# A last output sum in two column halves, sums moved ahead, and outputs behind an up product, in a RetNet and feed-forward kernel on one core

## The chip, the cores and the metric

The kernel runs on one core of a Trainium2 chip (trn2). The metric is the device time of one execution in microseconds (us); lower is better. The span in a profile is the time from the first to the last instruction; the measured time is some 1.8 us longer.

In the profile's lines PE is TensorE (matrix products), PEld its weight loads, DVE is VectorE, ACT is ScalarE, POOL is GpSimd and SP is SyncE; a name with q (SPq, ACTq) is that engine's issue of a transfer. In this kernel TensorE writes its products into banks of the memory PSUM; another engine copies them from there to a tile such as `sum` (0.69 us for VectorE's last copy, 128x512), and a transfer takes that to the output (256 KB land 2.0 us after issue, the median of 24). L462 is line 462 of the kernel that was run.

## The reference

A linear-attention recurrence makes rows of 512 numbers, and a feed-forward block with the activation `h - tanh(h)` follows:

```python
# q, k, v: 4 batches x 8 heads x 768 positions x 64, float32
for t in range(S):
    state = gamma * state + einsum('bhd,bhe->bhde', k[:, :, t], v[:, :, t])
    y[:, :, t] = scale * einsum('bhd,bhde->bhe', q[:, :, t], state)
x = y.transpose(0, 2, 1, 3).reshape(3072, 512)
h = x @ w_in                       # 512 x 2048
out = (h - tanh(h)) @ w_out        # 2048 x 512
```

## The kernel before

The positions are taken in 24 chunks of 128. The feed-forward part goes in 96 steps. A step is a tile `(n, m2)`: 256 rows `n` of x and 256 columns `m2` of the hidden layer. It has an "up" product into a PSUM bank, an activation of five ScalarE and six VectorE operations, and, two steps later (`LAG = 2`), a "down" product for each of two halves `j` of the rows. The down product adds up in a PSUM bank until the last tile of a group; then `add_up` empties the bank into the tile `sum`. The parts that the change touches:

```python
def shrink_multiply(n, m2):            # VectorE, three operations on h
    ...
def shrink_end(n, m2):                 # VectorE, three more; the last writes g
    ...

def down(n, m2, j, first, last):
    if first:
        o_p[j] = bank("o", f"o_{n}_{m2}_{j}")          # a pool of two banks
        keep_busy(o_p[j][:, :P])
    for i in range(2):
        nc.tensor.matmul(o_p[j], gT[n, m2][:, i, ts(j, P)], w2[:, 2 * m2 + i],
                         start=(first and i == 0), stop=(last and i == 1))

def add_up(n, m2, j):
    ...
    if j in begun:
        nc.vector.tensor_tensor(o, o_p[j], o, op=ALU.add)
    elif done and j % 2:
        nc.vector.tensor_copy(o, o_p[j])
    else:
        nc.scalar.copy(out=o, in_=o_p[j])
    begun.add(j)
    if done:
        nc.sync.dma_start(out=out[ds(n * TH + j * P, P)], in_=o)

def part(j, n, m2, first, last):
    down(n, m2, j, first, last)
    if last:
        add_up(n, m2, j)

def downs(lag):
    while len(waiting) > lag:
        tile_ = waiting.pop(0)
        for j in range(2):
            part(j, *tile_)

for s in range(BEGUN, len(steps)):
    n, m2, first, last = steps[s]
    ci = with_chunk.get(s)                 # every third step takes a chunk along
    if ci is not None:
        ...
        if ci >= FIRST:
            outputs_rest(ci)               # the chunk's last 16 small products into y
            keep_x(ci)                     # ScalarE: y -> xT
        if FIRST <= ci + 2 < NCH:
            products(ci + 2)
            mask(ci + 2)
            state(ci + 2)
        load_chunk(ci + 4)
        if FIRST <= ci + 1 < NCH:
            outputs(ci + 1)                # 48 small products into the same banks y
            see(ci + 1)
    ...
    for i in range(2):
        up(n, m2, i)
    waiting.append(steps[s])
    shrink_begin(n, m2)
    shrink_factors(n, m2)
    shrink_multiply(n, m2)
    shrink_end(n, m2)
    downs(LAG)
    ...
for j in range(2):
    for tile_ in waiting:
        part(j, *tile_)
```

## Time and profile before

| | before |
|---|---|
| device time, median of the first three runs | 755.27 us (754.33 to 755.91) |
| span of the profiled run | 752.6 us |
| TensorE busy | 739.6 us, 98% |
| VectorE, ScalarE busy | 69%, 52% |
| waits of TensorE after 100 us | three, 2.1 us together |

Two groups of instructions carry the kernel. The columns are line, engine, operation, tiles, shapes and count, then the busy time and the mean length of one in ns, then the idle time before them and what ended it:

```profile
L414 PE MATMUL h<-xT,w 128*128 128x256 f32 x1536 | 349.9, 381 | 0.3 <-DVE w L199 0.3
L462 PE MATMUL o<-w,g 128*128 128x512 f32 x768 | 345.6, 593 | 1.4 <-DVE sum L471 0.9 <-DVE g L453 0.5
```

They are the up and the down products, 695 of the 740 us. Each product written in the code is two rows here, since 96 steps with 8 up products make 768, not 1536. One row takes longer (381 ns) than its share of busy time (349.9 us / 1536 = 228 ns): they overlap. The last column is what a change can win without taking products away, and it is small. With TensorE at 98% there is little to win in the other engines' own time. What is left is the few spots where TensorE stands still, and the end, where everything else has to come after it.

### The profile page before, as it was taken

How to read it: one execution, taken by the hardware profiler on the slowest of the kernel's cores; microseconds unless marked ns; L12 is line 12 of the kernel's file. 1: busy time of each engine (PE TensorE's matmuls, PEld its weight loads, DVE VectorE, ACT ScalarE, POOL GpSimd, SP SyncE). 2: the span in 40 equal slices, each digit the busy share in tenths (PEclk: the TensorE clock that was granted, in tenths of full speed). 3: DMA queues.
4: the chain of work that ended last, by engine and by line, in shares of the span. 5: the costliest groups of instructions: out<-in, count | busy, mean ns of one | idle time of the engine just before them, and what ended most of it. 6: DMA issues, size and time to landing. Idle time of an engine off the chain costs nothing.

```text
span 752.6 us, 13801 instructions
## 1 busy us (share of the span) xinstructions
PE 739.6 (98%) x5470; PEld 501.9 (67%) x5470; DVE 518.7 (69%) x807; ACT 389.1 (52%) x725; POOL 125.9 (17%) x108
## 2 busy tenths in 40 slices
PE   7899999999999999999999999999999999999997
PEld 7786666666667676766676666666666666666663
DVE  4899889998898666656565656555665566556653
ACT  3667486666665545445545545444344434433441
POOL 0564445435453111100111100000000000000000
PEclk9999999999999999999999999999999999999999
DMA  9982546556553353332442422000000000000000
GB/s 191 231 204 59 127 99 180 149 148 160 149 128 91 92 140 115 88 82 78 106 99 74 96 57 58 28 1 1 29 0 1 28 1 0 29 0 1 28 2 28
DMA packets 125392, 59.76 MB, mean 79 GB/s; under 512 B 109840, under 2 KB 118160, under 8 KB 125328
## 3 DMA queue, kind: packets, MB, share of 16 engines
q1 hardware_dynamic: 125184, 58.73, 30.5%
q8 instruction: 43, 0.70, 0.4%
q10 hardware_dynamic: 144, 0.15, 0.1%
q14 instruction: 21, 0.17, 0.1%
HBM read 35.80 MB, written 14.68 MB: 67 GB/s over the span
## 4 chain that ended last, share of the span: by engine, by line
PE 94%; DVE 2%; DMA 1%; SPq 1%; ACT 1%; issue 1%; DVEq 0%; ACTq 0%
PE h L414 43%; PE o L462 43%; PE y L352 3%; PE s L298 2%; PE s L304 1%; DMA raws<-in_moe_w_in_dram 1%; PE kqTp L250 1%; DMA k<-in_k_dram 1%; SPq L229 1%; PE kqTp L212 0%; DVE head L185 0%; PE y L212 0%; SPq L154 0%; DVE head L183 0%; DVE g L453 0%
## 5 line engine op out<-in xcount | busy, mean ns | idle before, releaser
L414 PE MATMUL h<-xT,w 128*128 128x256 f32 x1536 | 349.9, 381 | 0.3 <-DVE w L199 0.3
L462 PE MATMUL o<-w,g 128*128 128x512 f32 x768 | 345.6, 593 | 1.4 <-DVE sum L471 0.9
L414 PEld LDWEIGHTS h<-xT,w 128*128 128x128 f32 x1536 | 289.7, 190 | 71.1 <-issue 34.0
L462 PEld LDWEIGHTS o<-w,g 128*128 128x128 f32 x768 | 145.4, 190 | 145.7 <-issue 136.6
L423 ACT ACTIVATE u<-h 128x512 f32<-128x512 f32 x96 | 57.3, 597 | 292.0 <-PE h L414 291.9
L439 DVE TENSOR_TENSOR th<-h,th 128x512 f32<-128x512 f32 x96 | 66.3, 690 | 176.0 <-ACT th L424 175.9
L453 DVE COPY_PREDICATED g<-large,th 128x512 f32<-128x512 int32 x96 | 72.1, 751 | 10.6 <-ACT apart L273 0.5
L442 DVE SCALAR_TENSOR_TENSOR h<-q,h 128x512 f32<-128x512 f32 x96 | 66.9, 696 | 10.4 <-DVE h L440 0.5
L448 DVE SCALAR_TENSOR_TENSOR h<-q,h 128x512 f32<-128x512 f32 x96 | 66.8, 696 | 9.9
L431 ACT ACTIVATE q<-u,tab 128x512 f32<-128x512 f32 x96 | 69.4, 723 | 0.0
L432 ACT ACTIVATE q<-u,tab 128x512 f32<-128x512 f32 x96 | 69.0, 718 | 0.0
L433 ACT ACTIVATE large<-u,tab 128x512 f32<-128x512 f32 x96 | 68.7, 716 | 0.0
L452 DVE TENSOR_TENSOR g<-h,u 128x512 f32<-128x512 f32 x96 | 66.3, 691 | 3.3
L440 DVE SCALAR_TENSOR_TENSOR h<-u,h 128x512 f32<-128x512 f32 x96 | 65.8, 685 | 0.0
L424 ACT ACTIVATE th<-h 128x512 f32<-128x512 f32 x96 | 56.8, 591 | 0.0
L236 POOL TENSOR_TENSOR q<-q,tab 128x512 f32<-128x512 f32 x22 | 23.2, 1057 | 199.7 <-DMA q<-in_q_dram 113.5
L195 POOL TENSOR_TENSOR low<-low,power 128x512 f32<-128x512 f32 x30 | 38.7, 1290 | 102.2 <-DVE power L187 80.6
L199 POOL TENSOR_TENSOR w<-low,head 128x512 f32<-128x512 f32 x30 | 38.5, 1284 | 2.4
L352 PEld LDWEIGHTS y<-a,v 64*64 64x64 f32 x768 | 15.8, 134 | 17.2 <-ACT large L433 10.6
L236 POOL TENSOR_TENSOR v<-v,tab 128x512 f32<-128x512 f32 x22 | 26.5, 1206 | 0.2 <-DMA v<-in_v_dram 0.2
L352 PE MATMUL y<-a,v 64*64 64x64 f32 x768 | 21.1, 224 | 2.3 <-issue 1.8
L382 ACT COPY seen<-y 64x1 f32<-64x1 f32 x96 | 10.1, 154 | 25.3 <-PE y L352 24.9
(49 smaller groups left out, 374.4 us busy)
## 6 DMA issues: line engine op xcount, KB each, us to landing
rows<-apart SPq DMA_DIRECT2D x16, 512.0 KB, 2.6
k<-in_k_dram SPq DMA_DIRECT2D x24, 256.0 KB, 4.0
q<-in_q_dram SPq DMA_DIRECT2D x24, 256.0 KB, 4.9
v<-in_v_dram SPq DMA_DIRECT2D x24, 256.0 KB, 5.3
raw<-in_moe_w_out_dram SPq DMA_DIRECT2D x12, 512.0 KB, 3.5
out_dram<-sum SPq DMA_DIRECT2D x24, 256.0 KB, 2.0
raw<-in_moe_w_in_dram SPq DMA_DIRECT2D x14, 256.0 KB, 4.2
raw<-in_moe_w_in_dram SPq DMA_DIRECT2D x28, 128.0 KB, 3.9
```

What stands on the lines that cost most here:

```text
L352: nc.tensor.matmul(y[ds(D * col, D), r, p // 2, ts(a, D)], lhsT, rhs, start=start, stop=True, skip_group_check=True)
L414: nc.tensor.matmul(hp, w1[:, c, ts(2 * m2 + i, P)], xT[n // 2][:, c, ts(n % 2, TH)], start=(i == 0 and c == 0), stop=(c == NC - 1), skip_g ...
L431: nc.scalar.activation(q0, u, AF.Square, bias=bias0)
L432: nc.scalar.activation(q1, u, AF.Square, bias=bias1, scale=math.sqrt(A))
L433: nc.scalar.activation(large, u, AF.Relu, bias=bias_m)
L439: nc.vector.tensor_tensor(th, hp, th, op=ALU.subtract)
L440: nc.vector.scalar_tensor_tensor(hp, in0=u, scalar=R, in1=hp, op0=ALU.subtract, op1=ALU.mult, reverse0=True)
L442: nc.vector.scalar_tensor_tensor(hp, in0=q0, scalar=C0, in1=hp, op0=ALU.add, op1=ALU.mult)
L448: nc.vector.scalar_tensor_tensor(hp, in0=q1, scalar=A * C1, in1=hp, op0=ALU.add, op1=ALU.mult)
L452: nc.vector.tensor_tensor(flat, hp, u, op=ALU.mult)
L453: nc.vector.copy_predicated(flat, large.bitcast(I32), th)
L462: nc.tensor.matmul(o_p[j], gT[n, m2][:, i, ts(j, P)], w2[:, 2 * m2 + i], start=(first and i == 0), stop=(last and i == 1))
```

## The change

The intent has four pieces. The sums are issued ahead of the activation's last three vector operations, so that PSUM banks come free sooner. The last chunk's outputs go behind an up product, so that this fills the wait for `keep_x`. At the end the waiting tiles are done one by one. And the second output sum of the last 256 rows is made in two column halves, each in its own bank, so that the first half can be copied and sent while the second is still being summed.

```diff
+    def down_half(n, m2, j, c, first, last):
+        if first and c == 0:
+            o_p[j] = banks("t", f"o_{n}_{m2}_{j}")       # one tile of two banks
+        for i in range(2):
+            nc.tensor.matmul(o_p[j][:, c, :TH], gT[n, m2][:, i, ts(j, P)],
+                             w2[:, 2 * m2 + i, ts(c, TH)],
+                             start=(first and i == 0), stop=(last and i == 1))
+
+    def store_half(n, j, c):
+        o = sums[n][0][:, j]
+        at = out[ds(n * TH + j * P, P)]
+        if c == 0:
+            nc.scalar.copy(out=o[:, :TH], in_=o_p[j][:, c, :TH])
+            nc.sync.dma_start(out=at[:, :TH], in_=o[:, :TH])
+            return
+        for quarter, copy, queue in (
+            (2, nc.vector.tensor_copy, nc.sync),
+            (3, nc.scalar.copy, nc.scalar),
+        ):
+            cols = ts(quarter, P)
+            copy(out=o[:, cols], in_=o_p[j][:, c, ts(quarter - 2, P)])
+            queue.dma_start(out=at[:, cols], in_=o[:, cols])
...
     def part(j, n, m2, first, last):
+        if n == 2 * NB - 1 and j == 1:
+            for c in range(2):
+                down_half(n, m2, j, c, first, last)
+                if last:
+                    store_half(n, j, c)
+            return
...
-            if FIRST <= ci + 1 < NCH:
+            if FIRST <= ci + 1 < NCH - 1:
                 outputs(ci + 1)
                 see(ci + 1)
...
             up(n, m2, i)
+        if ci == NCH - 2:
+            outputs(ci + 1)
+            see(ci + 1)
         waiting.append(steps[s])
...
         shrink_multiply(n, m2)
+        downs(LAG)
         shrink_end(n, m2)
-        downs(LAG)
...
-    for j in range(2):
-        for tile_ in waiting:
-            part(j, *tile_)
+    downs(0)
```

## The prediction

> **What bounds the kernel now.** I read the busy shares first, then the row of slices, then TensorE's waits, then the timeline around each wait.
>
> The page's busy shares and its TensorE row of 40 slices:
>
> ```profile
> PE 739.6 (98%) x5470; PEld 501.9 (67%) x5470; DVE 518.7 (69%) x807; ACT 389.1 (52%) x725; POOL 125.9 (17%) x108
> PE   7899999999999999999999999999999999999997
> ```
>
> TensorE is busy 98% of the span, at granted clock 1.0; only the first two and the last slice are below 9. So every microsecond that can be won without taking matmuls away is an idle spell of PE, and there are about 13 us of them (752.6 minus 739.6), mostly in the first 45 us, which the change doesn't touch. The view of PE's waits from 100 us to the end has only three entries (total, times, longest):
>
> ```profile
> PE o L462 <- DVE sum L471: 0.9, 1, 0.9
> PE y L352 <- ACT xT L393: 0.7, 1, 0.7
> PE o L462 <- DVE g L453: 0.5, 1, 0.5
> ```
>
> Each occurs once, and each part of the change aims at one. The timeline shows all three (start, length, engine, line, in brackets the idle time before). First, near 144 us:
>
> ```profile
> 139.83 3.62 PE L414 MATMUL h<-xT,w 128*128 128x256 f32 x16
> 142.95 0.73 DVE L453 COPY_PREDICATED g<-large,th 128x512 f32<-128x512 int32 x1
> 143.57 1.28 DVE L471 TENSOR_TENSOR sum<-o,sum 128x512 f32<-128x512 f32 x2
> 144.30 3.70 PE L462 MATMUL o<-w,g 128*128 128x512 f32 x8 [0.86 <-DVE sum L471]
> ```
>
> The new down product needs the PSUM banks that two sums still have to empty, and VectorE reaches these only after the last activation operation of the tile. Second, at the last chunk's outputs:
>
> ```profile
> 490.48 0.46 PE L352 MATMUL y<-a,v 64*64 64x64 f32 x16
> 491.01 0.59 ACT L393 COPY xT<-y 128x512 f32<-128x512 f32 x1 [0.94 <-PE y L352]
> 491.65 0.69 PE L352 MATMUL y<-kqT,state 64*64 64x64 f32 x32 [0.71 <-ACT xT L393]
> ```
>
> Earlier chunks have another chunk's products in this place; the last has none. Third, the end, with the row of output transfers (KB each, us from issue to landing) from the page:
>
> ```profile
> 737.68 5.31 PE L462 MATMUL o<-w,g 128*128 128x512 f32 x12
> 742.73 0.73 DVE L453 COPY_PREDICATED g<-large,th 128x512 f32<-128x512 int32 x1
> 743.51 5.42 PE L462 MATMUL o<-w,g 128*128 128x512 f32 x12 [0.51 <-DVE g L453]
> 748.96 0.69 DVE L473 COPY sum<-o 128x512 f32<-128x512 f32 x1 [5.51 <-PE o L462]
> out_dram<-sum SPq DMA_DIRECT2D x24, 256.0 KB, 2.0
> ```
>
> After PE ends (748.93) come 0.69 us of copy, a transfer issued at about 749.68 that lands 2.0 us later (751.65), and about 0.95 us of closing.
>
> [...]
>
> **The change part by part.** I also read the built program's list of instructions and waits of both kernels.
>
> *Sums ahead.* Same instructions, moved. In the step near 144 us the third activation operation ends at about 141.3; two sums of 0.68 us then end at about 142.7. PE wants the banks at 139.83 + 3.46 = 143.29 and began at 144.30. Gain 1.0 us, plus about 0.05 of restart. The activation tile comes later by up to 1.4 us in these steps, but is used two steps (more than 4 us) after it is due.
>
> *Outputs behind the up product.* Before, this spot costs 492.57 - 490.55 = 2.02 us between products of the main loop, plus 0.2 because an up product after small products takes 3.65 us and not 3.45: 2.22. After: the 16 small products cost 0.39 + 0.2 (as at 513.43 to 513.82); the 48 others, at 14.6 ns each (112 more products cost 1.64 us more at 467.7 to 469.7), cost 0.70, plus about 0.16 to enter and 0.2 to leave: 1.06. Sum 1.65. Gain 0.55 us.
>
> *The end.* Tile-wise order gives PE the second output of tile 6 to do while tile 7's activation ends. PE needs tile 7 at about 737.68 + 16 x 0.429 = 744.55, and it was ready at 743.46, so the 0.68 us of lost issue (743.51 minus 737.68 + 12 x 0.429) go, and PE unhindered would end at 748.25. But the list of waits holds a catch: the first product of the second half waits for ScalarE's semaphore at the count that the copy of the **first half** gives. The halves are in different banks of one tile, and PE stands still nonetheless. First half ends at 748.25 - 0.86 = 747.39; copy of 256 columns 0.02 + 0.37, wake 0.05, four passes of 216 ns and 0.19 of pipe: 748.88. PE's end hardly moves. Next, the list makes ScalarE's last quarter wait for VectorE's quarter [...]: 0.02 + 0.27 + 0.03 + 0.27 + 0.03, so the last transfer is issued at about 749.50, not 749.68. It carries 64 KB and not 256; I estimate 1.65 us to landing (a quarter of the bytes, in rows of 512 bytes, beside a twin): 751.15 instead of 751.65. Gain 0.5 us.
>
> *Split matmuls.* 8 tiles, each 8 passes of 216 ns for 4 of 429: 0.012 us each, so 0.1 us lost at most.
>
> Sum: 1.05 + 0.55 + 0.5 - 0.1 = 2.0 us. 755.27 - 2.0 = **753.3 us**.
>
> **The rivals.**
> R1, the end works as intended: PE doesn't stand still between the halves. Then it ends near 748.3, the quarters overlap, and the gain at the end is about 1.3 instead of 0.5: 752.4. For it: separate banks. Against it: the wait stands in the built program.
> R2, the wait turns up elsewhere: with sums ahead, VectorE blocks until the down product is complete, and the activation comes late. 17 later sum steps losing 0.3 us each would make 5 us, 758. For it: VectorE is at 8 to 9 tenths in slices 6 to 12. Against it: no step after 144 us shows any PE wait for an activation tile until the last one, so there is slack of steps, and PE's matmuls in these sums are nearly done when VectorE gets there.
> R3, small transfers land no sooner, or the last three queue behind each other (512 KB leave in about 2.5 us now, where the first 256 KB had 3.5 us of their own): last landing 2.0 us or more after issue, gain at the end 0 to 0.2, so 753.7.
> R4, half-width passes are slower than in the up product, by weight loads of 190 ns in a slot of 216: 25 ns on 64 passes are 1.6 us, 754.9. Against it: 16 up passes keep 216 with the same loads.
>
> **Range and chances.** The gains are 0.9 to 1.1, 0.3 to 0.7 and 0 to 1.3 us, which gives 752.4 to 754.1; three runs of the kernel before spread over 1.6 us, so I widen it to 752.0 to 754.8. Two per cent are 15 us; the idle spells the change can reach are 2.1 us of PE and some 3.7 us after it, so faster by 2% can't come about. Slower by 2% would need R2 at more than 0.5 us in every sum. Chances: 0.005 faster, 0.99 same, 0.005 slower.
>
> **What would show each step right or wrong.** PE's waits after 100 us should have lost the first two entries, and the one for the activation tile, and should have gained one of about 0.4 us: PE for ScalarE's copy of the half sum, near the end; without it R1 holds. The down product after the first sum should start 3.46 us after its up product. Last quarters: VectorE's, then ScalarE's, about 0.27 us each, end to end. The last transfer should land about 1.65 us after its issue; 2.0 or more is R3. Half-width passes of the down product spaced by more than 220 ns are R4. New PE waits for g or h between 150 and 500 us are R2, and would make the prediction wrong on the high side.

On the inputs of these sums: the spacing of the rows is from the chain of before, where an up product of 16 rows takes 3.45 us (216 ns a row of 256 columns) and a down product of 8 rows 3.43 us (429 ns a row of 512). The copy lengths for 128 and 256 columns (0.27 and 0.37 us) and the 1.65 us to landing were estimates. For the copies the trace of before can be asked: ScalarE's take 154 ns for one column (`seen`) and 582 for 512 (`sum`), VectorE's 418 for 256 (`state`) and 681 for 512, and straight lines through these give 0.26 and 0.37 us on ScalarE and 0.29 on VectorE. The changed kernel has 0.27 and 0.37 on ScalarE, 0.29 on VectorE, and 1.6 us to landing for 64 KB. That 64 KB would land sooner than the 2.0 us of 256 KB was not shown by the trace of before.

## The result

| | before | changed |
|---|---|---|
| median of 6 runs | 754.7 us (754.06 to 755.91) | 752.89 us (752.56 to 753.87) |
| span of the profiled run | 752.65 us | 752.06 us |

The ratio is 0.9977, with a 95% interval of 0.9964 to 0.9989. A ratio is the mean time of one kernel's fast runs over that of the other's in the same rounds, so it isn't quite the ratio of the medians in the table. All outputs are right.

The two profiled spans differ by 0.6 us only, the medians by 1.8. The profiled run of the changed kernel was the slowest of its six, and what it lost, it lost before the change acts. This is the table by stretches, for the stretch from 30 to 40 us (busy time and count for PE, PEld, DVE, ACT and POOL, then the granted TensorE clock, the DMA share and GB/s). First before, then changed:

```profile
30.00:40.00 10.00, 8.29 (x166) 7.29 (x167) 8.41 (x15) 6.27 (x14) 6.66 (x6) 1.00 0.91 253
```

```profile
30.00:40.00 10.00, 7.87 (x157) 7.10 (x158) 8.63 (x14) 5.74 (x13) 6.77 (x6) 0.83 0.83 241
```

The clock fell to 0.83 there. Both programs issue the same instructions in this stretch, so this differs by execution and not by kernel (in e5_apart and e8_apart_scalar below, whose clock stayed at 1.00, TensorE came to its main loop late as well, so the clock is not the whole cause). Why it fell is not shown; TensorE's longest idle spell there was 2.9 us. One and the same up product early in the main loop began at 132.94 us before and at 134.43 in the changed kernel. Over the ten profiles its start lies between 132.85 and 134.95 us. I therefore measure the effects from this product on: the **main stretch** from it to the start of the last up product, and the **end** from there to the end of the span.

| | main stretch | end | both, against before |
|---|---|---|---|
| before | 734.23 - 132.94 = 601.29 us | 18.42 us | |
| changed | 734.06 - 134.43 = 599.63 us | 18.00 us | 1.66 + 0.42 = 2.08 us less |

The end is read from the table by stretches, which gives it to 0.01 us; the span as the page prints it is rounded to 0.1 us. (The expectations below were written with ends taken from rounded spans, 18.37 and 18.04 us.) Before, then changed:

```profile
734.23:752.65 18.42, 14.18 (x41) 7.33 (x39) 6.92 (x10) 3.50 (x6) 0.00 (x0) 0.98 0.07 28
```

```profile
734.06:752.06 18.00, 14.22 (x53) 9.61 (x51) 6.53 (x10) 4.13 (x8) 0.00 (x0) 1.00 0.08 29
```

Each stretch comes from one profile per kernel. Kernels that are alike in a stretch agree closely there: the three with the end of before (18.40 to 18.42) and the three with the changed end (17.99 to 18.00) within 0.02 us, and the main stretches of five kernels with all of the change's main part within 0.01.

Now the lines that answer to those of before. The page's busy shares and TensorE's slices of the changed kernel:

```profile
PE 740.9 (99%) x5502; PEld 509.9 (68%) x5502; DVE 518.0 (69%) x807; ACT 389.4 (52%) x727; POOL 126.9 (17%) x108
PE   8899999999999999999999999999999999999997
```

TensorE has 32 rows more (5502 against 5470), the halves. The view of its waits from 100 us to the end has one entry in place of three:

```profile
PE o L470 <- ACT sum L478: 0.5, 1, 0.5
```

The timeline at the first sum:

```profile
141.31 3.62 PE L414 MATMUL h<-xT,w 128*128 128x256 f32 x16
142.71 1.28 DVE L495 TENSOR_TENSOR sum<-o,sum 128x512 f32<-128x512 f32 x2
143.91 0.69 DVE L448 SCALAR_TENSOR_TENSOR h<-q,h 128x512 f32<-128x512 f32 x1
...
144.77 1.45 PE L462 MATMUL o<-w,g 128*128 128x512 f32 x3
```

The sums (L495 now) end before the up product does, and the down product follows 3.46 us after the up product began; before it was 4.47. The timeline at the last chunk's outputs:

```profile
490.84 0.46 PE L352 MATMUL y<-a,v 64*64 64x64 f32 x16
491.23 3.72 PE L414 MATMUL h<-xT,w 128*128 128x256 f32 x16
491.37 0.58 ACT L393 COPY xT<-y 128x512 f32<-128x512 f32 x1 [0.94 <-PE y L352]
...
494.88 0.69 PE L352 MATMUL y<-kqT,state 64*64 64x64 f32 x32
```

ScalarE's copy to xT now lies inside the up product, and there is no bracket at the second row of small products. The end:

```profile
744.40 1.88 PE L462 MATMUL o<-w,g 128*128 128x512 f32 x4
746.12 1.03 PE L470 MATMUL o<-w,g 128*128 128x256 f32 x4
...
747.18 0.37 ACT L478 COPY sum<-o 128x256 f32<-128x256 f32 x1 [0.28 <-PE o L470]
...
747.61 1.13 PE L470 MATMUL o<-w,g 128*128 128x256 f32 x4 [0.46 <-ACT sum L478]
748.83 0.29 DVE L486 COPY sum<-o 128x128 f32<-128x128 f32 x1 [5.54 <-DMA out_dram<-sum]
...
749.15 0.27 ACT L486 COPY sum<-o 128x128 f32<-128x128 f32 x1 [1.60 <-DVE sum L486]
749.45 0.35 ACTq L487 DMA_DIRECT2D out_dram<-sum  x1
```

The last tile no longer waits for its activation. In its place there is a new wait in the middle of the last output: the second half (L470 at 747.61) starts only when ScalarE has copied the first (747.18 + 0.37). The two last quarters are copied one after the other, 748.83 and 749.15, on two engines. (For the bracket at 748.83 the profile names a transfer as the releaser. The last one issued before, at 746.93, took 2.0 us and landed only after the copy had begun, so it can't have released it; the copy follows TensorE's end at 748.74.)

### The profile page after: what moved, and what is told of

Its sections match the earlier page's. It is cut to its first block, busy times and chain, and to the rows that moved or that the text cites. A ratio compares the mean times of both kernels' runs of the same rounds, so it can differ in the third digit from the quotient of the medians.

```text
span 752.1 us, 13885 instructions
## 1 busy us (share of the span) xinstructions
PE 740.9 (99%) x5502; PEld 509.9 (68%) x5502; DVE 518.0 (69%) x807; ACT 389.4 (52%) x727; POOL 126.9 (17%) x108
## 4 chain that ended last, share of the span: by engine, by line
PE 96%; DMA 2%; DVE 1%; SPq 1%; ACT 0%; issue 0%; ACTq 0%; DVEq 0%
PE h L414 44%; PE o L462 42%; PE y L352 3%; PE o L470 2%; PE s L298 2%; PE s L304 1%; PE kqTp L212 1%; PE kqTp L250 1%; DMA raw<-in_moe_w_in_dram 1%; DMA k<-in_k_dram 1%; SPq L229 1%; DMA out_dram<-sum 0%; SPq L154 0%; DVE power L187 0%; DVE head L185 0%; DVE a L311 0%
## 5 line engine op out<-in xcount | busy, mean ns | idle before, releaser
L462 PE MATMUL o<-w,g 128*128 128x512 f32 x736 | 331.9, 593 | 0.0
L462 PEld LDWEIGHTS o<-w,g 128*128 128x128 f32 x736 | 139.4, 190 | 135.1 <-issue 128.4
L393 ACT COPY xT<-y 128x512 f32<-128x512 f32 x24 | 14.1, 587 | 17.0 <-PE y L352 17.0
```

## The experiments

The first four kernels ran on one chip and share nine runs of the kernel before (median 754.76 us), and the last four likewise (754.8 us). Since a start that differs by up to 2 us lies on every time, I read each effect from the profile's stretches, and use the times as a check.

**e1_sums**: the kernel before, with the sums moved alone.

```diff
-        shrink_end(n, m2)
         downs(LAG)
+        shrink_end(n, m2)
```

> The kernel before with the sums moved ahead of the activation's last three operations, and nothing else. Theory (the sum of independent gains): the idle spell of 0.86 us at the first sum goes, the down product there starts 3.46 us after its up product and not 4.47; the other two late waits of PE (0.7 for the xT copy, 0.5 for the activation tile at the end) stay. Time 1.0 us less than before, ratio about 0.9987. Rival (VectorE blocks in its sums and hands its waits on): the wait is gone but new PE waits for g or h turn up between 150 and 500 us, and the time is the same as before or longer.

Median 753.3 us of 5, ratio 0.9985 (0.9973 to 0.9998). The first wait is gone, the other two are there, and no new one came. The main stretch is 733.04 - 132.87 = 600.17 us, 1.12 less than before; the end is 18.40, as before within 0.02. The rival falls.

**e2_outputs**: the kernel before, with the last chunk's outputs moved alone.

```diff
-            if FIRST <= ci + 1 < NCH:
+            if FIRST <= ci + 1 < NCH - 1:
...
+        if ci == NCH - 2:
+            outputs(ci + 1)
+            see(ci + 1)
```

> The kernel before with only the last chunk's outputs moved behind an up product. Theory: the wait of 0.71 us for the xT copy goes, but the small products leave a dense stretch twice instead of once (0.2 us each), so the stretch from the down product before to the one after is shorter by 0.55 us and not by 0.9. Time 0.55 us less, ratio about 0.9993. Rival (the whole wait is won): 0.7 us or more less in that stretch.

Median 754.34 us of 5, ratio 0.9996 (0.9984 to 1.0009): as a time, inconclusive. The profile is not. The chain of work that ended last (start, length, what) shows the spot before:

```profile
490.55 0.44 PE y L352 x16
...
491.65 0.93 PE y L352 x48
492.57 3.65 PE h L414 x16
496.23 3.43 PE o L462 x8
499.66 3.45 PE h L414 x16
```

and in this run:

```profile
492.13 0.39 PE y L352 x16
492.52 3.65 PE h L414 x16
496.17 0.86 PE y L352 x48
497.03 3.63 PE o L462 x8
500.66 3.45 PE h L414 x16
```

From the first small products to the next step's up product it takes 500.66 - 492.13 = 8.53 us, against 499.66 - 490.55 = 9.11. So 0.58 us are won of a wait of 0.71. The rest is seen in the lengths: the down product took 3.43 us when it followed an up product and takes 3.63 after small ones. The rival, the whole wait, falls. The main stretch is 600.71 us, 0.58 less than before.

**e3_end**: the kernel before, with only the end changed (`downs(0)`, `down_half` and `store_half`).

```diff
-    for j in range(2):
-        for tile_ in waiting:
-            part(j, *tile_)
+    downs(0)
     # and part(), down_half(), store_half() as in the change
```

> The kernel before with only the end changed: tile by tile order and the last output in two halves. Theory: from the start of the last up product to the end of the span 18.0 us as in the changed kernel, against 18.37 before; PE's wait for the copy of the first half is there with about 0.5 us. Time 0.35 us less than before, ratio about 0.9995. Rival (the end works as meant and the rest of the change is worth little): 17.4 us or less, and the time 1 us less.

Median 754.45 us of 5, ratio 0.9998 (0.9985 to 1.0012). As a time this is inconclusive. The end is 17.99 us, 0.43 less than before, and has the wait for the first half, 0.5 us. The main stretch is 601.38 us, 0.09 longer, about what six steps with half-width products were expected to cost. The whole end is thus worth 0.34 us, and the rival falls.

**e4_whole**: the changed kernel, with the last output kept whole.

```diff
-        if n == 2 * NB - 1 and j == 1:
+        if False and n == 2 * NB - 1 and j == 1:
```

> The changed kernel with the last output kept whole (512 columns, one copy, one transfer of 256 KB); sums, outputs and the tile by tile order stay. Theory (the halves cost a PE stall of about 0.6 us and the last quarters run one after the other, so the halves win nothing): from the start of the last up product to the end 17.75 us, 0.3 us less than the changed kernel's 18.04; time the same as the changed kernel's or 0.3 us less. Rival (the halves carry the gain at the end): 18.4 us or more, time 0.5 us or more above the changed kernel's.

Median 752.82 us of 5, ratio 0.9975 (0.9962 to 0.9987). The main stretch is 732.89 - 133.30 = 599.59 us; that is 1.70 less than before, and the 1.12 and 0.58 of the first two runs add up to it. The end is 17.63 us. Its timeline:

```profile
736.34 10.46 PE L462 MATMUL o<-w,g 128*128 128x512 f32 x24
...
746.84 0.69 DVE L497 COPY sum<-o 128x512 f32<-128x512 f32 x1 [4.73 <-PE o L462]
```

All 24 rows run without a gap, and one copy and one transfer follow. This end is 0.37 us shorter than that of the changed kernel. The tile-wise order alone brings 18.42 - 17.63 = 0.79 us; the halves, as built, give 0.37 of it back. In the times this is too small to be seen (0.9975 against 0.9977).

**e5_apart**: the changed kernel, with the halves in two PSUM tiles.

```diff
-        if first and c == 0:
-            o_p[j] = banks("t", f"o_{n}_{m2}_{j}")
+        if first:
+            o_half[c] = banks("t", ...)[:, 0] if c == 0 else bank("o", ...)
```

> The changed kernel with the two column halves in two separate PSUM tiles (the second in a bank of the pool of the whole outputs, free by then) instead of two banks of one tile; copies and transfers as in the changed kernel. Theory (the stall between the halves comes from the wait kept for the tile, not from the banks): PE's 0.5 us wait for the copy of the first half is gone, PE's last product ends 0.73 us sooner, and from the start of the last up product to the end it takes 17.3 us (17.5 if the transfers get in each other's way) against 18.04. Rival (the end is held by the transfers, not by PE): the wait is gone, but that stretch stays above 17.9 us.

Median 752.18 us of 5, ratio 0.9963 (0.995 to 0.9975). TensorE has no wait after 100 us. The timeline of the end:

```profile
745.41 1.03 PE L472 MATMUL o<-w,g 128*128 128x256 f32 x4
...
746.27 1.03 PE L472 MATMUL o_1b<-w,g 128*128 128x256 f32 x4
746.48 0.37 ACT L480 COPY sum<-o 128x256 f32<-128x256 f32 x1 [0.28 <-PE o L472]
...
747.34 0.29 DVE L488 COPY sum<-o_1b 128x128 f32<-128x128 f32 x1 [4.75 <-PE o_1b L472]
```

The second half starts 0.86 us after the first (1.49 in the changed kernel), and ScalarE copies the first half while the second is being summed. The end is 17.20 us, 0.80 shorter than the changed kernel's and 0.43 shorter than with the output whole. The rival, that transfers hold the end, falls.

**e6_apart_single**: the same, but the second half leaves in one VectorE copy and one transfer.

```diff
-        for quarter, copy, queue in (...):        # two copies, two transfers
-            ...
+        nc.vector.tensor_copy(o[:, TH:], o_half[c][:, :TH])
+        nc.scalar.dma_start(out=at[:, TH:], in_=o[:, TH:])
```

> As the run with separate tiles, but the second half leaves in one VectorE copy of 256 columns (about 0.42 us) and one transfer of 128 KB instead of two quarters on two engines. Theory (the quarters run one after the other, 0.29 + 0.27 and 0.03 between[...]; and 128 KB land only 0.1 us later than 64): the stretch from the last up product to the end is the same as with quarters within 0.1 us, 17.2 to 17.3. Rival (two engines and two queues are worth something): 0.25 us or more longer than with quarters.

Median 751.72 us of 5 (751.49 to 751.87), ratio 0.9958 (0.9945 to 0.997). The end is 17.19 us, the same as with quarters (17.20). Two engines and two queues were worth nothing here: one copy took 0.42 us where two in turn take 0.29 + 0.03 + 0.27, and 128 KB landed 1.7 us after issue where 64 KB took 1.6. Why the program lets the second quarter's copy wait for the first was not tested: the two share a bank, and also a PSUM tile.

**e7_sums_first**: the changed kernel, with the sums still further ahead.

```diff
+        downs(LAG)
         shrink_multiply(n, m2)
-        downs(LAG)
         shrink_end(n, m2)
```

> The changed kernel with the sums moved further ahead, before all six vector operations of the activation. Theory (the activation tile has about 4 us of slack, but VectorE is nearly full until 300 us): VectorE stands waiting for the down product in each sum step, about 3 us; after 300 us, where it is half idle, PE still waits for nothing; before 300 us VectorE falls behind and PE waits between 1 and 15 us in all. Rival (there is no slack to speak of, and the sums as changed were just lucky): PE waits in the seven late sum steps too, and the time is 10 us or more above the changed kernel's.

Median 753.22 us of 4, ratio 0.9974 (0.9959 to 0.9989). My expectation for the time before 300 us was wrong: TensorE has no wait at all after 100 us but the one between the halves. The view of VectorE's waits from 50 us on shows what the place of the sums costs that engine:

```profile
DVE sum L497 <- PE o L462: 34.5, 7, 6.0
DVE sum L495 <- PE o L462: 19.2, 12, 3.5
```

VectorE stands for 53.7 us in its sums, and all of it is hidden. (In the changed kernel the same two rows have 1.6 us together.) The main stretch is 599.64 us, the changed kernel's within 0.01. The rival, that there is no slack, falls with even more room than I had given the theory.

**e8_apart_scalar**: as e6_apart_single, with VectorE on the first half and ScalarE on the second.

```diff
-            nc.scalar.copy(out=o[:, :TH], in_=o_half[c][:, :TH])      # c == 0
-        nc.vector.tensor_copy(o[:, TH:], o_half[c][:, :TH])           # c == 1
+        cols = ts(c, TH)
+        (nc.vector.tensor_copy, nc.scalar.copy)[c](out=o[:, cols], in_=o_half[c][:, :TH])
+        (nc.sync, nc.scalar)[c].dma_start(out=at[:, cols], in_=o[:, cols])
```

> As the run with one copy and one transfer for the second half, but VectorE copies the first half and ScalarE the second (0.37 us, against about 0.42 on VectorE, and it issues the transfer itself). Theory: 0.05 to 0.15 us shorter at the end than with VectorE, 17.1 to 17.2 us from the last up product; time 1.0 us less than the changed kernel's, 0.9962 of the kernel before. Rival (the end is set by the first transfers, 256 and 128 KB, still under way): no difference.

Median 752.14 us of 5 (751.66 to 752.55), ratio 0.9963 (0.9951 to 0.9976). The end is 17.11 us, 0.08 less than with VectorE's copy, as expected; the rival falls, if by little. The time was not lower. In the two profiled runs (752.44 and 751.49 us) the later start, 133.88 against 132.85 at the product that I measure from, is more than the difference; that the start parts the medians too is not shown. By profile this is the best end; by time e6_apart_single is the best kernel. Which of the two is better stays open, since the start varies by more than what parts them. Both beat the kernel before (intervals below 1) and have a shorter end than the changed one.

The stretches of all runs, in us:

| | main stretch | end | less than before, both | ratio of times |
|---|---|---|---|---|
| before | 601.29 | 18.42 | | 1 |
| changed | 599.63 | 18.00 | 2.08 | 0.9977 |
| e1_sums | 600.17 | 18.40 | 1.14 | 0.9985 |
| e2_outputs | 600.71 | 18.42 | 0.58 | 0.9996 |
| e3_end | 601.38 | 17.99 | 0.34 | 0.9998 |
| e4_whole | 599.59 | 17.63 | 2.49 | 0.9975 |
| e5_apart | 599.64 | 17.20 | 2.87 | 0.9963 |
| e6_apart_single | 599.64 | 17.19 | 2.88 | 0.9958 |
| e7_sums_first | 599.64 | 18.00 | 2.07 | 0.9974 |
| e8_apart_scalar | 599.64 | 17.11 | 2.96 | 0.9963 |

## Why the prediction was right

The measured 752.89 us lies in the range, 0.4 us from the figure. By itself that shows little: the median of before, 754.7, lies in the range of 752.0 to 754.8 too. What bears the prediction out is the profile, where the mechanism held part by part.

- *Sums ahead*: 1.05 us were expected, 1.12 measured (e1_sums). The wait went and did not turn up elsewhere; R2 fell (it counted 17 later sum steps; the trace has 15 in which VectorE sums), and e7_sums_first showed much more slack than the prediction claimed.
- *Outputs*: 0.55 expected, 0.58 measured. The point was to subtract the second change between small and full-size products; the 0.71 of the wait alone would have been too much.
- *The end*: 0.5 expected, 0.42 measured. The wait between the halves came where the program's list of waits had put it (0.46 us of idle time, second half complete at 748.74, expected at 748.88 in the time of before or 748.71 in that of the changed run). The quarters ran in turn. What was mis-sized is the sum after TensorE's end: VectorE's copy began 0.09 us after it and not 0.02, and took 0.29 and not 0.27 us. With the 0.03 that TensorE ended late, the last transfer went out at 749.45, 0.12 later than the sum gives in that run's time. The landing was sized well: 1.6 us, expected 1.65. R1 and R3 fell; with the wait taken away (e5_apart) the end gained 1.22 us, near the 1.3 that R1 had named.
- *Half-width products*: at most 0.1 expected, 0.09 measured in e3_end and 0.04 between the changed kernel and e4_whole (main stretch alone). A last output of a tile took 1.73 us in halves (739.23 to 740.96) and 1.72 whole. R4 fell.
- The figure was 0.4 us above the measured median although the sum of the parts (2.0) is nearly what the profile shows (2.08). Most of that is the starting point: the expectation started from the first median of before, 755.27, and three more runs brought that to 754.7. The rest is within the spread of the runs.

What the prediction did not see is the size of what the halves cost: it had the loss in it, but it did not say that leaving the output whole would be better, as e4_whole shows.

## What to carry to other kernels

When a split is meant to let one engine read what another is done with, look in the built program for the wait that this needs to be free of: here two banks of one tile still counted as one (TensorE stood for 0.46 us between the halves), and two tiles were worth 0.8 us where the split as built lost 0.4. Where the busiest engine is at 98% and its work stays the same, look for the gain in its few idle spells and in what follows its last product, less what entering and leaving each filler costs. Measured from a point after the noisy start, parts of tenths of a microsecond added up within a few hundredths here (e1_sums, e2_outputs and e3_end 2.06 us together, the whole change 2.08). Splitting a last copy over two engines and two queues gained nothing here, where the program made the second copy wait for the first and 64 KB landed only 0.1 us sooner than 128 KB.

## Lengths and clocks that these runs show

- At the end of the profiled runs, transfers of `sum` to the output, issued by SyncE or ScalarE, landed 1.6 us after issue for 64 KB, 1.7 to 1.8 for 128 KB and 2.0 to 2.1 for 256 KB. My estimate from 64 and 256 KB is a fixed part of about 1.5 us (0.4 us for 192 KB more, so 0.13 us of the 1.6 for the first 64); it leaves out that the smaller transfers also have shorter rows.
- Copies from PSUM to `sum` took 292, about 420 and 681 to 692 ns on VectorE for 128, 256 and 512 columns, and 265, 372 and about 580 ns on ScalarE.
- With the halves in two banks of one tile TensorE stood for 0.46 us (changed kernel, e3_end, e7_sums_first), and with two tiles it had no wait after 100 us (e5_apart, e6_apart_single, e8_apart_scalar). The wait stands in the built program's list; these runs don't show that the chip needs it.
- In the profile of e3_end the clock was 0.50 from 18 to 20 us; TensorE's waits just before were of 1.05 and 0.68 us, with products between them. In four of ten profiles the clock fell somewhere in the first 50 us, in the other six it did not. What makes it fall is not shown.
- A change between 64x64 and full-size products cost 0.2 us each time at the last chunk's outputs (an up product of 3.65 us and not 3.45, a down product of 3.63 and not 3.43).
